# Loads of the first two pairs issued from ScalarE's queue as well as SyncE's, in a fused linear-attention and gated-MLP kernel

## The chip, the cores and the metric

The kernel runs on one core of a Trainium2 chip. The metric is device time in microseconds (us). A core has a matrix engine (TensorE, in the profile PE; its weight loads are PEld), a vector engine (VectorE, DVE), an engine for activation functions (ScalarE, ACT), GpSimd (POOL) and SyncE (SP), which here only starts transfers. Each engine runs its own instructions in order. A transfer (DMA) is started by an instruction on an engine's queue and then carried by 16 DMA engines.

## The reference

The first half is a recurrence over 768 time steps for 4 batches and 8 heads, with a state of 48 by 48 that decays per row; the second is a two-layer network on the result, with the activation h * cos(h).

```python
for t in range(S):                       # q, k, v, alpha: [4, 8, 768, 48], float32
    state = alpha[:, :, t, :, None] * state + einsum('bhd,bhe->bhde', k[:, :, t], v[:, :, t])
    y[:, :, t] = einsum('bhd,bhde->bhe', q[:, :, t], state)
x = y.transpose(0, 2, 1, 3).reshape(3072, 384)
h = x @ w_in                             # [384, 2048]
return (h * cos(h)) @ w_out              # [2048, 384], float32
```

## The kernel before

Time is cut into 12 pairs (J = 0 to 11, three for each batch) of 256 steps. A partition holds two neighbouring steps (e = 0 and 1) of all heads, and each half of the partitions is a chunk of its own. For each pair the kernel

- loads a (alpha), k, q and v, each as a tile of 128 partitions with 8 heads of 96 float32 (`load`, L102 to L116; one transfer of 384 KB each),
- takes the logarithm of a on ScalarE (`ln`, L139), sums it over time on PE by matmuls with triangular masks (`cums0` and `cums`, L155 and L167) and takes exponentials of the sums and of their negatives on ScalarE (`exps`, L200, and `icp`, L192),
- scales k and q by these (`scale_k`, L212, `scale_q`, L216), casts v to bfloat16 (`cast_v`, L219) and copies it into a second layout (`stack_v_pe`, L235, `evict_vs`, L239),
- forms the outer products that feed the state (`outer`, L291), transposes q and k (`trans`, L260, `evict_T`, L266), forms scores (L274), masks them (L279), and builds y (`yT`, L340),
- runs the network: `mlp1` (L359), the cosine on ScalarE (`cosine`, L365), the product on VectorE (`gate`, L370), `mlp2` (L387), the copy out of PSUM and the store.

The logarithm and exponential share one set of ScalarE's function tables, the cosine has another; `act_set` (L136) loads the first set where it isn't in place.

All steps are issued in an order that is written out by hand. `PLAN` has a line for each kind of step and on it a number for each pair; the steps are sorted by these numbers and issued in that order, so the numbers set the order of the instructions on every engine, and nothing else. A suffix gives the engine (A for ScalarE, D for VectorE). Before the change the loads of pairs 0 and 1 stand in the order k0, a0, a1, k1, v0, q0, q1, v1, all on SyncE's queue. `IDLE` puts matmuls on zeros (`idle`, L411) into PE's order, 21 of them at its start. The loads of pair 2 and later stand on SyncE's queue as well; the load of a for pair 2 waits for `yT` of pair 1 (`GATES`). The weights w1 and w2 are loaded from GpSimd's queue (L121, L127).

Of the kernel before, what the change touches and what calls it, by code (L numbers as in the profile page):

```python
# [16 lines left out]
def kernel(  # L17
# [10 lines left out]
    nc = tc.nc  # L28
# [73 lines left out]
    def load(nm, J):  # L102
        b, g = J // NJB, J % NJB
        t = sb.tile([C, H, 2, D], FP, tag=nm, name=nm, bufs=BUF["a" if nm == "a" else "in"])
        dma = nc.sync.dma_start(
            out=t.rearrange("p h e d -> p h (e d)"),
            in_=src[nm][b, :, g * T2 : (g + 1) * T2, :].rearrange("h (p e) d -> p h (e d)", e=2),
        )
        if (nm, J) in AFTER:
            tc.add_manual_dep(dma.ins, AFTER[nm, J].ins.name,  # L110
                              mybir.DependencyInfo(mybir.DependencyClass.Sync, mybir.DependencyReason.DATA),
                              reason="inputs of later pairs stay behind the weights")
        if nm == "a":
            a_sb[J] = t
        else:
            kqv[nm, J] = t  # L116
# [290 lines left out]
    def idle(n):  # L407
# [6 lines left out]
    mults = {"DVE": nc.vector, "POOL": nc.gpsimd}  # L414
    steps = {
        "load": lambda J, nm: load(nm, J), "w1": load_w1, "w2": load_w2,
        "mula": mul_a, "ln": ln, "cums0": cums0, "cums": cums, "sub": sub, "icp": icp, "exps": exps, "eb": session,
        "sk": lambda J, e, eng="POOL": scale_k(J, e, mults[eng]), "sq": lambda J, e, eng="POOL": scale_q(J, e, mults[eng]),
# [7 lines left out]


    PLAN = {
        "load a": "1320 1974 27415 27985 34270 40270 43270 54870 67336 68770 70970 93397",
        "load k": "750 2544 28555 37270 46270 52480 58570 69470 72470 85140 91627 113474",  # L430
        "load q": "5250 6750 29125 38770 48970 56370 57870 60070 78470 84570 87104 96187",
        "load v": "3750 8250 35770 41770 51910 61570 67906 73970 75470 85710 95267 96757",
        "w1": "15334 12769 17804 16954",
        "w2": "11919 20284 19434 21134",
        "mula": "- - - 36680 41180 47582 54280 61956 76220 87867 79850 105765",
# [61 lines left out]
    for key, line in PLAN.items():  # L497
        kind, *rest = key.split()
        for J, word in enumerate(line.split()):
            if word != "-":  # L500
                t, _, eng = word.partition(":")
# [38 lines left out]
```

## Time and profile before

| | |
|---|---|
| median of 3 runs | 189.61 us (189.58 to 190.51) |
| profiled execution: its own time | 189.73 us |
| profiled execution: span from first to last instruction | 187.7 us |
| mean granted TensorE clock | 0.997 of full speed |
| busy: PE, DVE, ACT, POOL | 177.2, 134.3, 125.3, 77.4 us |
| data moved | 29.47 MB, a mean of 157 GB/s |

The profile is of one execution. A line of a timeline has the start, the time taken, the engine, the line of the code, the operation with its output and input tiles, the number of instructions that are merged, and in brackets how long the engine had been idle before it and what released it. SPq and ACTq are the issuing instructions of a queue, and their time is that of the issue, not of the transfer. A line of the chain of waits has a start, a time and the work that the end of the program goes back to at that moment. A line of the DMA view with a queue's name has packets, megabytes and the share of 16 DMA engines.

### The profile page before, as it was taken

What the parts mean: (1) busy time and instruction counts of PE and PEld (TensorE: products, weight loads), DVE (VectorE), ACT (ScalarE), POOL (GpSimd) and SP (SyncE); (2) the same over time, 40 slices, a digit from 0 to 9 for tenths busy, and PEclk for the clock granted to TensorE, in tenths of its full rate; (3) what the DMA queues carried; (4) which work ended last, traced back from release to release, by engine and by line L of the source; (5) the groups of instructions that cost most, each with busy time, mean ns of one, the idle gap of its engine ahead of it and who ended that gap; (6) DMA issues with size and microseconds to landing.
All of it is one profiled execution on the core that took longest, in us unless ns stands there. A gap on an engine that the chain in (4) does not pass through costs nothing.

```text
span 187.7 us, 5795 instructions
## 1 busy us (share of the span) xinstructions
PE 177.2 (94%) x2471; PEld 126.7 (67%) x2474; DVE 134.3 (72%) x184; ACT 125.3 (67%) x161; POOL 77.4 (41%) x110
## 2 busy tenths in 40 slices
PE   7997799998999999999999999999999999999990
PEld 2444678664577776775688668686776786776880
DVE  7069775589799899589657986885876666573550
ACT  2466876899598977788577999728956182372520
POOL 5059610257664733783894068830540310100000
PEclk9999999999999999999999999999999999999998
DMA  6999999999959988996799943600042005501303
GB/s 152 261 256 154 185 203 236 255 264 265 249 137 302 265 184 217 265 268 166 195 280 259 216 106 90 166 0 3 3 114 73 0 21 124 128 1 45 84 0 84
DMA packets 60537, 29.47 MB, mean 157 GB/s; under 512 B 51424, under 2 KB 60512, under 8 KB 60512
## 3 DMA queue, kind: packets, MB, share of 16 engines
q1 hardware_dynamic: 56640, 25.86, 59.8%
q0 software_dynamic: 3712, 3.15, 11.0%
q8 instruction: 19, 0.31, 0.7%
q10 hardware_dynamic: 160, 0.10, 0.2%
q14 instruction: 6, 0.05, 0.1%
HBM read 25.17 MB, written 4.72 MB: 159 GB/s over the span
## 4 chain that ended last, share of the span: by engine, by line
PE 71%; ACT 16%; DVE 7%; issue 3%; DVEq 0%
PE h_ps L359 31%; PE o_ps L387 23%; PE idle_ps L411 5%; PE y_ps L340 3%; ACT c_sb L365 3%; ACT qkT L266 3%; DVE gsb L370 3%; PE T_ps L260 2%; ACT cp L200 2%; ACT L136 2%; ACT L365 2%; PE A_ps L274 2%; PE U_ps L291 2%; ACT lna L141 2%; ACT icp L192 2%
## 5 line engine op out<-in xcount | busy, mean ns | idle before, releaser
L370 DVE TENSOR_TENSOR gsb<-h_ps,c_sb 128x1024 bf16<-128x1024 f32 x48 | 58.1, 1221 | 22.3 <-ACT c_sb L365 21.5
L365 ACT ACTIVATE c_sb<-h_ps,halfpi 128x1024 bf16<-128x1024 f32 x48 | 53.0, 1113 | 27.4 <-PE h_ps L359 23.4
L359 PE MATMUL h_ps<-xT,w 128*128 128x256 bf16 x576 | 66.7, 273 | 1.4 <-issue 0.6
L387 PE MATMUL o_ps<-w,gsb 128*128 128x384 bf16 x368 | 66.7, 326 | 0.0
L359 PEld LDWEIGHTS <-w 128*128 128x128 bf16 x576 | 55.6, 98 | 10.4 <-issue 1.9
L387 PEld LDWEIGHTS <-gsb 128*128 128x128 bf16 x368 | 33.8, 98 | 21.2 <-DVE gsb L370 0.6
L313 POOL TENSOR_TENSOR un<-us,c 128x384 bf16<-128x384 f32 x20 | 16.8, 843 | 40.3 <-DVE us L305 33.9
L279 DVE TENSOR_TENSOR A_sb<-A_ps,msk 128x1024 bf16<-128x1024 f32 x24 | 28.9, 1216 | 1.3 <-PE A_ps L274 1.3
L212 POOL TENSOR_TENSOR kh<-k,icp 128x384 bf16<-128x384 f32 x17 | 16.9, 999 | 8.7 <-ACT icp L192 8.7
L216 POOL TENSOR_TENSOR qh<-q,cp 128x384 bf16<-128x384 f32 x15 | 15.4, 1032 | 10.9 <-ACT cp L200 10.9
L149 POOL TENSOR_TENSOR a<-a 128x384 f32<-128x384 f32 x9 | 9.3, 1037 | 12.9 <-DMA a<-in_alpha_dram 12.9
L411 PE MATMUL idle_ps<-zeros 128*128 128x512 bf16 x42 | 12.7, 445 | 1.6 <-DVE zeros L52 1.2
L219 POOL CAST vp<-v 128x768 bf16<-128x768 f32 x12 | 9.9, 824 | 9.0 <-DMA v<-in_v_dram 8.9
L141 ACT ACTIVATE lna<-a 128x768 bf16<-128x768 f32 x12 | 10.2, 846 | 4.5 <-DMA a<-in_alpha_dram 4.5
L136 ACT ACT_TABLE_LOAD x9 | 11.5, 1283 | 0.9 <-PEq L524 0.7
L266 ACT COPY qkT<-T_ps 128x1024 bf16<-128x1024 bf16 x8 | 8.0, 1016 | 6.2 <-PE T_ps L260 3.8
L266 DVE COPY qkT<-T_ps 128x1024 bf16<-128x1024 bf16 x16 | 10.8, 682 | 1.3 <-ACT qkT L266 1.3
L365 ACT ACT_TABLE_LOAD x9 | 11.5, 1283 | 0.2
L305 DVE TENSOR_TENSOR us<-U_ps,un 128x384 f32<-128x384 f32 x16 | 8.7, 550 | 3.8 <-PE U_ps L291 2.8
L396 DVE COPY o_sb<-o_ps 128x384 f32<-128x384 f32 x12 | 6.6, 552 | 6.6 <-PE o_ps L387 6.6
L274 PE MATMUL A_ps<-qkT 48*128 48x128 bf16 x192 | 9.2, 218 | 1.0 <-ACT vs L239 0.6
L396 ACT COPY o_sb<-o_ps 128x384 f32<-128x384 f32 x11 | 5.3, 478 | 7.1 <-PE o_ps L387 5.2
(69 smaller groups left out, 155.1 us busy)
## 6 DMA issues: line engine op xcount, KB each, us to landing
k<-in_k_dram SPq DMA_DIRECT2D x12, 384.0 KB, 5.5
a<-in_alpha_dram SPq DMA_DIRECT2D x12, 384.0 KB, 5.9
v<-in_v_dram SPq DMA_DIRECT2D x12, 384.0 KB, 6.2
q<-in_q_dram SPq DMA_DIRECT2D x12, 384.0 KB, 6.0
out_dram<-o_sb SPq DMA_DIRECT2D x46, 96.0 KB, 2.7
vs<-vp SPq DMA_DIRECT2D x36, 64.0 KB, 2.0
w<-in_moe_w_out_dram POOLq DMA_DIRECT2D x4, 384.0 KB, 9.9
w<-in_moe_w_in_dram POOLq DMA_DIRECT2D x4, 384.0 KB, 7.0
```

Source lines behind the costliest of these rows:

```text
L136: nc.scalar.preload_act_table_set("natural_log_exp_and_others")
L141: nc.scalar.activation(out=lna_t[J % NL][:, :, :, 0:D].rearrange("p e h d -> p h e d"), in_=a_sb.pop(J), func=AF.Ln)
L212: eng.tensor_tensor(out=kh_t[J % NQ][:, e, :, 0:D], in0=kqv["k", J][:, :, e], in1=icp_, op=ALU.mult)
L216: eng.tensor_tensor(out=qh_t[J % NQ][:, e, :, 0:D], in0=kqv["q", J][:, :, e], in1=cp, op=ALU.mult)
L266: copy(out=qkT_sb[J][:, c], in_=T_ps[J][:, c].rearrange("r n e s -> r n (e s)"))
L279: nc.vector.tensor_tensor(out=A_sb[J][:, c].rearrange("s a p t -> s (a p) t"), in0=A_ps.pop((J, c)).rearrange("s a p t -> s (a p) t"), in1 ...
L313: nc.gpsimd.tensor_tensor(out=u, in0=U_sum.pop(n), in1=c2_sb[J][:, :, c].unsqueeze(3).to_broadcast([C, NP, 2, D]), op=ALU.mult)
L359: nc.tensor.matmul(h_ps[J, u][:, f, :], w1[:, kk, ft * C : (ft + 1) * C], xT[J][:, kk, :], start=(kk == 0), stop=(kk == KT - 1))
L365: nc.scalar.activation(out=c_sb[J, u], in_=h_ps[J, u], func=AF.Sin, bias=halfpi, scale=1.0)
L370: nc.vector.tensor_tensor(out=gsb[J][:, u * FW : (u + 1) * FW], in0=h_ps.pop((J, u)), in1=c_sb.pop((J, u)), op=ALU.mult)
L387: nc.tensor.matmul(o_ps[J, c][:, 0:DM], gsb[J][:, ft, c * C : (c + 1) * C], w2[:, ft], start=(ft == 0), stop=(ft == NF - 1))
L411: nc.tensor.matmul(idle_ps[0], zeros[:, 0:C], zeros, start=True, stop=True)
```

## The change

The first two pairs' k and v are issued from ScalarE's queue, and all eight loads of these pairs get numbers at the head of the plan, in the order k0, a0, k1, a1, v0, q0, v1, q1. In the sorted order the four on ScalarE's queue then stand ahead of the first step that uses ScalarE, and with it ahead of its first table load. All other steps keep their numbers.

```diff
     def load(nm, J):
         b, g = J // NJB, J % NJB
         t = sb.tile([C, H, 2, D], FP, tag=nm, name=nm, bufs=BUF["a" if nm == "a" else "in"])
-        dma = nc.sync.dma_start(
+        eng = nc.scalar if J < 2 and nm in "kv" else nc.sync
+        dma = eng.dma_start(
             out=t.rearrange("p h e d -> p h (e d)"),
             in_=src[nm][b, :, g * T2 : (g + 1) * T2, :].rearrange("h (p e) d -> p h (e d)", e=2),
         )
...
-        "load a": "1320 1974 27415 27985 34270 40270 43270 54870 67336 68770 70970 93397",
-        "load k": "750 2544 28555 37270 46270 52480 58570 69470 72470 85140 91627 113474",
-        "load q": "5250 6750 29125 38770 48970 56370 57870 60070 78470 84570 87104 96187",
-        "load v": "3750 8250 35770 41770 51910 61570 67906 73970 75470 85710 95267 96757",
+        "load a": "752 754 27415 27985 34270 40270 43270 54870 67336 68770 70970 93397",
+        "load k": "751 753 28555 37270 46270 52480 58570 69470 72470 85140 91627 113474",
+        "load q": "756 758 29125 38770 48970 56370 57870 60070 78470 84570 87104 96187",
+        "load v": "755 757 35770 41770 51910 61570 67906 73970 75470 85710 95267 96757",
```

## The prediction

> **What bounds the kernel now.** The page comes first: PE is busy for 94% of the span and the granted clock is at 9 tenths or more up to the last slice, so a change at the start counts if it moves the moment from which PE runs without pause. I therefore read the chain of waits for the first 28 us.
>
> ```profile
> 1.20 7.00 PE idle_ps L411 x21
> 8.19 0.65 PE cums_h L155 x4
> 8.84 0.18 PE cums_h L167 x8
> 9.02 0.24 PE idle_ps L411
> 9.26 0.65 PE cums_h L155 x4
> 9.91 0.19 PE cums_h L167 x8
> 10.10 0.02 issue
> 10.13 0.49 ACT cp L200
> 10.62 0.39 ACT icp L192
> 11.01 0.02 issue
> 11.03 1.10 DVE kh L212 x2
> ```
>
> No transfer is in it. The 21 filler matmuls hold PE until 8.2 us, then the cumulative sums of pair 0 and pair 1 follow, and ScalarE's second exponential (10.13) waits for pair 1's sums. From there to the end of the span the chain is computation. So earlier data cannot shorten it; later data can lengthen it. How late may data be? The next view is the timeline of ScalarE and of SyncE's queue.
>
> ```profile
> 0.74 1.28 ACT L136 ACT_TABLE_LOAD   x1 [0.74 <-PEq L524]
> 5.86 0.84 ACT L141 ACTIVATE lna<-a 128x768 bf16<-128x768 f32 x1 [3.83 <-DMA a<-in_alpha_dram]
> 7.36 0.84 ACT L141 ACTIVATE lna<-a 128x768 bf16<-128x768 f32 x1 [0.67 <-DMA a<-in_alpha_dram]
> ...
> 0.74 0.42 SPq L105 DMA_DIRECT2D k<-in_k_dram  x1
> 1.23 1.60 SPq L105 DMA_DIRECT2D a<-in_alpha_dram  x2
> 2.87 1.25 SPq L105 DMA_DIRECT2D k<-in_k_dram  x1
> 4.16 1.44 SPq L105 DMA_DIRECT2D v<-in_v_dram  x1
> 5.65 2.93 SPq L105 DMA_DIRECT2D q<-in_q_dram  x2
> 8.62 1.44 SPq L105 DMA_DIRECT2D v<-in_v_dram  x1
> ```
>
> The logarithm of pair 0 ends at 6.70 and is used at 8.03; that of pair 1 ends at 8.20 and is used at 9.10. The slack is 1.33 and 0.90 us. The table load is over at 2.02, well ahead of the first data.
>
> The queue's lines show something else: an issue takes 0.42 us when nothing is queued, but 1.25 to 1.44 from the third or fourth on. The issuing engine is held. The DMA view, cut at the ends of the fourth, fifth and sixth issue (4.12, 5.60 and 7.10 us), shows why:
>
> ```profile
> q1 hardware_dynamic: 1486, 0.56, 53.5%
> q1 hardware_dynamic: 2508, 0.95, 72.9%
> q1 hardware_dynamic: 3546, 1.34, 84.4%
> ```
>
> A load is 1,024 packets of 384 bytes. Issued less moved is 4096 - 1486 = 2610, then 5120 - 2508 = 2612, then 6144 - 3546 = 2598: the queue takes about 2,600 packets (2.5 loads) and the next issue ends only as packets leave. They leave at (3546 - 2508) / 1.5 = 692 per us, 262 GB/s, one load each 1.5 us. Issue start plus time to landing gives the landings: k0 4.36, a0 5.8, a1 7.3, k1 8.87, v0 10.4, q0 11.85, q1 13.3, v1 14.8.
>
> **What the change does, part by part.** In the compiled order ScalarE begins with k0, k1, v0, v1, and only then come the table load and the two logarithms. SyncE begins with a0, a1, q0, q1. Engine orders on PE, VectorE and GpSimd stay as they were. Nothing is added or removed in work; eight issues are spread over two queues, and ScalarE gets four of them ahead of its first computation.
>
> *The transfers.* The bytes are the same and the stretch 4 to 10 us already runs at 261 to 262 GB/s, so the last of the eight lands at about 14.8 as before. The order changes. Both queues begin at 0.74 and have equal loads, so I take them to fill the stream in turn: k0 with a0, k1 with a1, v0 with q0, v1 with q1, each couple landing at the time of the later one. Then a0 5.8 as now, a1 8.87 instead of 7.3, k0 and k1 early enough (k is first used at 9.58), v0 11.85 instead of 10.4, q0 as now, q1 14.8 instead of 13.3. The bounds for a1 are its old place (7.3) and the fourth place (8.87); equal sharing is nearest to the fourth, and I take it. The Trainium skill says the same of the gain, against the change: in "DMA: Bandwidth & Descriptors", section "Issuing engines are not separate DMA queues", DMAs from any engine run on the same 16 DMA engines and interleave, and a second issuer saves only sequencer time. By that rule the stream would stay at its 262 GB/s, as the sum has it; no run here yet shows two load queues together.
>
> *ScalarE's time.* If its queue can hold 2,600 packets of its own, v1's issue ends when 4096 - 2600 = 1,496 packets of this queue have left. With equal shares that is 2,992 in all, at 5.60 + (2992 - 2508) / 692 = 6.30 us. The table load (1.28, nothing hides it now) ends at 7.6, pair 0's logarithm at 8.44. PE has been ready for it at 8.03, so pair 0's sums are 0.43 late and end, with the one filler matmul, at 8.46 + 1.07 = 9.53. Pair 1's logarithm starts on a1 at 8.87 and ends at 9.71; its sums start at 9.73 instead of 9.10. That is +0.63, and it covers the 0.43.
>
> *What follows.* Pair 1's sums release ScalarE's second exponential at 10.76 instead of 10.13. The products kh, on VectorE, end at 12.76 instead of 12.13. GpSimd's cast of v0 starts on v0 at 11.87 and takes 0.82: 12.70, so PE's outer products, which need both, begin at 12.78; the two of them that ran ahead at 11.77 now run here, about 0.02. VectorE's product for pair 1's q, 14.37 before, comes at 15.0, behind q1's 14.8. GpSimd's weight issues stand behind the cast and two small products, and go 0.6 later along with their users (the first weight matmul is at 22.25). The sum is +0.65 us. Below, +0.43 (a1 early, ScalarE the limit); above, +0.9 (ScalarE's fourth issue also waits for one of SyncE's, or the shared stream loses some rate). The chain behind it has no slack that would give it back.
>
> The profiled execution took 189.73 with a span of 187.7, 0.12 over the median of 189.61. From its span the forecast is 188.35 us, and from the median 190.26: 190.3.
>
> **The rivals.**
>
> *One shared allowance: much slower.* The 2,600 packets could be the limit of both queues together. The issues then end as in the SyncE column now, in turn, and ScalarE's fourth is the seventh or the eighth: 8.58 or 10.06. Add the table load (1.29) and pair 0's logarithm (0.84): PE starts the sums at 10.74 or 12.2 instead of 8.03, +2.71 or +4.2, nothing in between hides it, and the time is 192.3 or 193.8. It decides as soon as v1's issue ends later than about 6.7. For it: the trace has one queue only under load, so whose limit it is stays unseen. Against it: the page counts the two queues apart (q1 and q10), and at 183.8 to 184.5, where SyncE and ScalarE both issue stores, ScalarE's took 565 and 550 ns and SyncE's 547 to 717, against a median of 595 for all SyncE's stores; neither stood behind the other for a whole issue. The Trainium skill speaks for it: "Perfetto Trace Analysis", section "DMA Instruction — HWDGE (DVE, Sync)", has one descriptor generator shared by the sequencers and locked until an issue's descriptors are all made. A full lock of this kind is not what the store rows show. I give the case 30 in 100: 17 for the seventh place, 13 for the eighth. In between (a partly shared limit, +0.95 to +2.4) I put 7.
>
> *Hidden: no change.* If SyncE's queue is served first, a1 keeps its old landing, and if ScalarE's fourth issue ends by 5.9, its table load and logarithms lie inside the slack: 189.6. It needs both; 4 in 100.
>
> *Faster.* Two queues could draw more than 262 GB/s. But the page's best slices are 302 and 280, and the chain's start is filler matmuls, not data; a gain over 0.95 us would have to come from a better order later on, for which no row speaks: 188.6 or less, 4 in 100.
>
> **How the numbers follow.** The forecast has 55 in 100, with its own range from 190.0 to 190.5; 3 of the 55 lie above the half per cent. A measurement of this kernel tells about 0.5% from no change, 0.95 us here, so the forecast itself is a slowdown that counts as the same. Same: 52 + 4 = 56. Slower: 3 + 30 + 7 = 40. Faster: 4. The range leaves out the eighth place (13) and the faster case (4): from 189.6 to 192.9, which takes in the seventh place with 0.6 for its error.
>
> **What would show it.** In the profile after, ScalarE's queue should have four issues from 0.74, the last ending at 6.3 to 6.7; the table load behind it; the logarithms at about 7.6 and 8.87, the second still waiting for a; the second exponential at 10.76; the weight matmuls from 22.9. If the fourth issue ends at 8.5 or later and the second logarithm follows the first without a wait, the shared allowance is right and the price is ScalarE's. If the logarithms are at 5.9 and 7.4, the change is hidden. A total below 189 would make the whole reading of the start wrong.

## The result, and the profile after

The changed kernel takes 191.93 us (median of 4 runs, 191.65 to 192.72) against 189.88 for the kernel before (4 runs), a ratio of 1.0115 with a 95% interval of 1.0084 to 1.0147: 1.2% slower, 2.05 us. Timed again later beside other kernels it gave 1.0124 (1.0092 to 1.0155). The forecast was 190.3, with a range from 189.6 to 192.9. The direction held; the size was a third of the measured one. By the prediction's own line of 0.5% between the same and slower this is slower, to which it gave 40 in 100 and not the larger share. That the range held is partly luck: its upper part was there for the rival of one shared allowance, which did not come true, and the forecast's own range, 190.0 to 190.5, missed.

The profiled execution of the change has a span of 190.9 us at its own time of 192.72, the longest of its four; the other three have spans of 189.9 to 190.2. First the timeline of SyncE's queue and of ScalarE in the changed kernel (start, time taken, engine, line, operation, tiles):

```profile
0.75 1.07 SPq L106 DMA_DIRECT2D a<-in_alpha_dram  x2
1.86 3.96 SPq L106 DMA_DIRECT2D q<-in_q_dram  x2
...
0.74 1.25 ACTq L106 DMA_DIRECT2D k<-in_k_dram  x2
2.02 4.48 ACTq L106 DMA_DIRECT2D v<-in_v_dram  x2
6.53 1.28 ACT L137 ACT_TABLE_LOAD   x1 [6.53 <-issue]
7.82 1.64 ACT L142 ACTIVATE lna<-a 128x768 bf16<-128x768 f32 x2
9.74 0.49 ACT L193 ACTIVATE icp<-cums_h 128x384 f32<-128x384 f32 x1 [0.28 <-PE cums_h L168]
10.81 0.49 ACT L201 ACTIVATE cp<-cums_h 128x384 f32<-128x384 f32 x1 [0.58 <-PE cums_h L168]
```

ScalarE's four issues end at 6.50, the table load follows at 6.53, and the second exponential starts at 10.81 instead of 10.13. That is the forecast almost to the tenth (6.3 to 6.7, and 10.76). The two logarithms run without a wait between them, though; the forecast had the second one wait for its a.

Next, the chain of waits of the changed kernel from the second exponential to the first weight matmul (start, time, what):

```profile
10.81 0.49 ACT cp L201
11.30 0.39 ACT icp L193
11.69 0.02 issue
11.71 0.80 DVE kh L213 x2
12.51 0.14 issue
12.65 1.18 DVE kh L213
13.83 0.97 DVE qh L217 x2
14.80 0.47 DVE us L308
15.27 1.67 DVE qh L217 x2
16.94 0.68 issue
17.62 0.56 DVE us L306
18.17 0.14 issue
18.31 0.40 PE A_ps L275 x8
...
24.21 0.04 issue
24.25 2.79 PE h_ps L360 x24
```

Before, the chain went through PE and ScalarE here; now it goes through VectorE. One product kh takes 1.18 us, where such a product took about 0.55; the second state sum (L306) starts at 17.62 instead of 15.95, and the scores of pair 0, which wait for it, at 18.31 instead of 16.30. The first weight matmul is at 24.25 instead of 22.25: here the loss stands at 2.00 us.

The scores did not wait for this sum before. These are the scores, ScalarE's copy of v into the second layout (`evict_vs`) and the second state sum, first in the kernel before and then in the changed one:

```profile
15.44 0.81 ACT L239 CAST vs<-vs_ps 128x768 bf16<-128x768 f32 x1
15.95 0.54 DVE L305 TENSOR_TENSOR us<-U_ps,un 128x384 f32<-128x384 f32 x1
16.30 0.40 PE L274 MATMUL A_ps<-qkT 48*128 48x128 bf16 x8 [0.62 <-ACT vs L239]
...
16.77 0.81 ACT L240 CAST vs<-vs_ps 128x768 bf16<-128x768 f32 x1
17.62 0.55 DVE L306 TENSOR_TENSOR us<-U_ps,un 128x384 f32<-128x384 f32 x1
18.31 0.40 PE L275 MATMUL A_ps<-qkT 48*128 48x128 bf16 x8 [1.31 <-DVE us L306]
```

Before, the scores started 0.05 us after the copy, while the sum still ran; after, 0.14 us behind the sum, and the copy had long been done. The kernel's code lets the tiles U_ps, vs_ps, T_ps and A_ps take turns in three PSUM buffers (tag "h", `bufs=3`), so the scores seem to have got another of them, although every engine computes in the same order as before. Why the build chose so is open. The profiles fall into two groups. In the kernel before and in experiments 3 and 8 the scores wait for the copy; in the changed kernel and in experiments 1, 2, 4, 5, 6 and 7 they wait for the sum. From the scores to the first weight matmul it is 5.94 to 5.95 us in all of them, so the whole loss is there when the scores start. By these rows the copy is 1.3 us late; the wait for the sum in its place makes the other 0.7, an estimate (18.31 against 17.58 + 0.05).

What GpSimd did at that time, in its timeline:

```profile
12.56 0.86 POOL L220 CAST vp<-v 128x768 bf16<-128x768 f32 x1 [9.38 <-DMA v<-in_v_dram]
13.39 1.00 POOL L245 TENSOR_TENSOR c<-cp,dmask 128x16 f32<-128x16 f32 x2
14.34 0.93 POOL L128 DMA_DIRECT2D w<-in_moe_w_out_dram  x1
15.26 0.75 POOL L122 DMA_DIRECT2D w<-in_moe_w_in_dram  x1
16.02 0.85 POOL L314 TENSOR_TENSOR un<-us,c 128x384 bf16<-128x384 f32 x1
```

The cast waits for pair 0's v until 12.56 (10.42 before), and from then on GpSimd is never free until the state product `un` at 16.02, which was at 14.61. PE's outer products wait for this cast (13.47, where most of them stood at 12.18 before; PE is idle for 0.95 us ahead of them), and the copy of v stands behind them on PE and ScalarE.

Behind 24.25 the distance stays between 2.0 and 2.5 until 98 us. There PE pauses in mid-layer with no releaser (0.62 us before, 1.36 after), which makes the 3.2 us of the two profiled spans. That pause differs from one execution to the next, from 0.6 to 1.6 in most of the profiles below and absent in one; the 2.05 of the medians is nearly the 2.00 of the first 24 us.

### The profile page after: what moved, and what is told of

Same layout as the page of the kernel before. It is cut to its first block, busy times and chain, and to the rows that moved or that the text cites. A ratio compares the mean times of both kernels' runs of the same rounds, so it can differ in the third digit from the quotient of the medians.

```text
span 190.9 us, 5796 instructions
## 1 busy us (share of the span) xinstructions
PE 177.3 (93%) x2471; PEld 126.7 (66%) x2474; DVE 136.2 (71%) x184; ACT 125.3 (66%) x161; POOL 77.1 (40%) x110
## 3 DMA queue, kind: packets, MB, share of 16 engines
q10 hardware_dynamic: 4320, 1.67, 4.1%
## 4 chain that ended last, share of the span: by engine, by line
PE 61%; ACT 12%; DVE 9%; DMA 5%; issue 4%; ACTq 3%; SPq 2%; POOL 2%; POOLq 0%; DVEq 0%
PE h_ps L360 27%; PE o_ps L388 22%; DMA v<-in_v_dram 5%; PE y_ps L341 3%; ACTq L106 3%; DVE gsb L371 3%; ACT c_sb L366 2%; DVE qh L217 2%; PE A_ps L275 2%; ACT L137 2%; PE T_ps L261 2%; DVE kh L213 2%; ACT qkT L267 2%; PE U_ps L292 1%; ACT cp L201 1%
## 5 line engine op out<-in xcount | busy, mean ns | idle before, releaser
L306 DVE TENSOR_TENSOR us<-U_ps,un 128x384 f32<-128x384 f32 x16 | 8.7, 550 | 3.8 <-PE U_ps L292 2.8
L213 DVE TENSOR_TENSOR kh<-k,icp 128x384 bf16<-128x384 f32 x7 | 5.2, 765 | 7.2 <-ACT icp L193 7.2
```

The lines of the kernel that those rows point to most:

```text
L213: eng.tensor_tensor(out=kh_t[J % NQ][:, e, :, 0:D], in0=kqv["k", J][:, :, e], in1=icp_, op=ALU.mult)
```

## The experiments

Two theories went in. **Late operands**: ScalarE's late logarithms cost 0.7, the late landing of pair 0's v more, and the work beside it on VectorE and GpSimd the rest. **ScalarE held**: all of it comes from ScalarE being kept by its own issues until 6.5. Each kernel was timed against the kernel before; "weights at" is the start of the first weight matmul in its profile (before 22.25, changed 24.25).

**1. The table load ahead of the four issues** (the changed kernel with one line more)

```diff
+        act_set("exp")
         for _, _, kind, args in sorted(order, key=lambda x: x[:2]):
```

> The changed kernel with ScalarE's table load moved ahead of its four load issues. Theory 'late v': the change costs its 2.0 us in three steps, ScalarE held until 6.5 (+0.7 at the second exponential), pair 0's v landing at 12.5 instead of 10.4 so that the outer products start at 13.47 instead of 12.18, and the cast of that v then running beside VectorE's products, which take longer (+0.7). The table load is hidden here, but the four issues start 1.3 us later, so v lands no earlier: outer products at 13.5 to 14.2, time 191.6 to 192.5. Rival 'ScalarE held': all of the loss comes from ScalarE's logarithms starting late; they start at 6.5 to 7.2 here, inside or near the old slack, and the time falls to 189.9 to 190.4.

Measured 191.64 us, ratio 1.0067 (1.0044 to 1.0090); weights at 24.01. ScalarE's timeline:

```profile
0.74 1.28 ACT L137 ACT_TABLE_LOAD   x1 [0.74 <-PEq L526]
0.78 1.21 ACTq L106 DMA_DIRECT2D k<-in_k_dram  x2
2.02 4.52 ACTq L106 DMA_DIRECT2D v<-in_v_dram  x2
6.58 0.84 ACT L142 ACTIVATE lna<-a 128x768 bf16<-128x768 f32 x1 [4.56 <-issue]
8.69 0.84 ACT L142 ACTIVATE lna<-a 128x768 bf16<-128x768 f32 x1 [1.27 <-DMA a<-in_alpha_dram]
```

The issues did not start later, as I had expected: they run beside the table load. So the table load is hidden and pair 0's logarithm is 1.2 us earlier, yet pair 1's waits for its a until 8.69 and the second exponential comes at 10.61 instead of 10.81. Of the 0.68 us at this point, 0.2 belong to ScalarE's issues and 0.5 to a1, which stands behind k0 and k1 in the shared stream. The cast of v was still at 12.70. "ScalarE held" falls: it expected 189.9 to 190.4.

**2. Half of the queues: only k on ScalarE's**

```diff
-        eng = nc.scalar if J < 2 and nm in "kv" else nc.sync
+        eng = nc.scalar if J < 2 and nm == "k" else nc.sync
```

with SyncE's loads in the order a0, a1, v0, q0, q1, v1 (two numbers of the plan changed for it).

> Half of the change: only the two loads of k on ScalarE's queue; SyncE's has a0, a1, v0, q0, q1, v1. ScalarE's issues should end near 2.0 and the table load near 3.3. Late v: v0 is the third on SyncE's queue and lands near 10, the logarithms are not held, 189.5 to 190.4. ScalarE held: the same, as ScalarE is free early. A third rival, 'two queues slow the stream' (two load queues move less per us than one): v0 and the later loads land later than 10.4 and the time is above 190.5.

Measured 190.65, ratio 1.0014 (0.9992 to 1.0035); weights at 23.21. ScalarE's two issues end at 1.98 and its table load at 3.29. The cast of v0 starts at 10.73. That is later than 10.4 and the time is above 190.5, as the third rival said, but the stream was not slower: from 6 to 12 us it moved 261 to 262 GB/s, as in the kernel before (261). The second exponential is at 10.75, since a1's logarithm started only at 8.71. The time is a little over the expected 190.4; the scores waited for the state sum here, until 17.27, 0.34 us longer than for the copy of v (16.88) by the same reckoning as above.

**3. The order alone, all on SyncE's queue**

```diff
-        eng = nc.scalar if J < 2 and nm in "kv" else nc.sync
+        eng = nc.sync
```

> The other half of the change: the eight loads in the new order k0, a0, k1, a1, v0, q0, v1, q1, but all on SyncE's queue, so ScalarE issues nothing. a1 lands at 8.87 instead of 7.3 and v0 at 10.4 as before. Late v: second exponential at 10.7 to 10.8 because of a1 (+0.63), outer products at 12.8, time 190.3 to 190.9. ScalarE held: 189.9, the same as before, since ScalarE is not held by issues.

Measured 190.80, ratio 1.0021 (0.9996 to 1.0045); weights at 23.15. a1's logarithm starts at 9.11, the second exponential at 11.03, the cast of v0 at 10.66 as early as ever. So putting k1 ahead of a1 costs 0.90 us at the first weight matmul without any second queue; about 0.2 of it is a start of the whole stream that was later in this profile (a0's logarithm at 6.09 instead of 5.86). The medians put it at 0.6 with an interval that touches zero.

**4. v0 and q0 exchanged between the queues** (ScalarE issues as many loads)

```diff
-        eng = nc.scalar if J < 2 and nm in "kv" else nc.sync
+        eng = nc.scalar if (nm, J) in (("k", 0), ("k", 1), ("q", 0), ("v", 1)) else nc.sync
```

The two loads have each other's number in the plan as well.

> The changed kernel with the queues of pair 0's v and q exchanged: SyncE has a0, a1, v0, q1 and ScalarE k0, k1, q0, v1, so ScalarE issues as many loads as in the change and is held as long (to 6.5), while v0 stands third on the queue that got ahead. Late v: v0 lands near 10.7 instead of 12.5, outer products at 12.85 instead of 13.47, and GpSimd's cast is over before most of VectorE's products: 190.4 to 191.2. ScalarE held: no change against the changed kernel, 191.7 to 192.2.

Measured 191.07, ratio 1.0032 (1.0011 to 1.0053); weights at 23.53. ScalarE's issues end at 6.63, as late as in the change, and its logarithms start at 7.95; the cast starts at 11.95, 0.6 earlier than in the change (10.7 had been expected), and 0.7 of the 2.0 us at the first weight matmul are back. The interval of the ratio lies below that of the change, and "ScalarE held", which expected 191.7 to 192.2, falls here too.

**5. The changed kernel again, and its second state sum ahead of one product**

> The changed kernel itself, timed beside the next three on the same chip: 191.6 to 192.2 and a ratio to the kernel before of 1.007 to 1.011.

Measured 192.39, ratio 1.0124 (1.0092 to 1.0155), a little above both expectations.

```diff
-        "sq 0": "12160:D 14753:D 40150:D ...
+        "sq 0": "12160:D 15560:D 40150:D ...
```

> The changed kernel with one VectorE product (pair 1's q, e = 0) moved behind the second state sum of pair 0 (L306). In the profile of the change this product took 2.04 us beside GpSimd's work instead of 0.55, and the state sum behind it, which frees the PSUM buffer that the scores of pair 0 wait for, started at 17.62 although its operand from GpSimd was there at 16.87. Theory 'late operands' with a collision on the path: the sum starts at 16.9, the scores at 17.6 instead of 18.31, and the time falls by 0.4 to 0.7 against the changed kernel. Rival 'off the path' (the scores wait for something else as well): less than 0.2.

Measured 191.62, ratio 1.0098 (1.0062 to 1.0133): the intervals overlap, so this run does not decide. In its profile the scores are at 18.17 against 18.55 in the repeat of the change, with the cast at 12.76 and 12.80. But the encounter of the cast with kh fell the other way round here: the cast took 1.22 us and the three products kh 1.50 together, where the change has 0.86 and 2.12. With the longer cast the copy of v ended only at 18.13, so the scores could hardly have come earlier by either wait.

**6. v0 late, without a second queue** (the kernel before with pair 0's q and v exchanged; one queue, a1 where it was)

```diff
-        "load q": "5250 6750 ...
+        "load q": "3750 6750 ...
-        "load v": "3750 8250 ...
+        "load v": "5250 8250 ...
```

> The kernel before, all loads on SyncE's queue, with pair 0's v and q exchanged: v lands sixth, near 11.87, instead of fifth, near 10.4. ScalarE issues nothing and a1 lands as before. Late operands: GpSimd's cast starts at 11.9, the outer products at 12.75 instead of 12.18, and the time rises by 0.5 to 0.9. Rival 'ScalarE and a1 alone': v has room until 11.3 at least and what is lost is given back, within 0.2 of the kernel before.

Measured 191.38, ratio 1.0086 (1.0054 to 1.0119): 1.2 us by the medians and 1.6 by the ratio, more than the 0.5 to 0.9 us expected. The chain of waits:

```profile
10.26 0.49 ACT cp L200
...
12.10 1.18 DVE kh L212
13.28 0.97 DVE qh L216 x2
14.26 0.47 DVE us L307
14.72 1.67 DVE qh L216 x2
16.39 0.68 issue
17.07 0.56 DVE us L305
17.62 0.14 issue
17.76 0.40 PE A_ps L274 x8
```

The second exponential is at 10.26, 0.13 after that of the kernel before (its whole start is 0.12 later). From kh on, the chain has the durations of the changed kernel one for one: 1.18, 0.97, 0.47, 1.67, and the pause ahead of the state sum. The cast started at 12.03 here, beside the product kh at 12.10. Weights at 23.71, +1.46. A cast 1.6 us later, on the old queue, with ScalarE untouched, brings three quarters of the loss. It does so in the same two parts: the outer products are at 12.92 and the copy of v ends at 17.02, 0.8 later than before, which is what had been expected; the scores start 0.7 after that, because in this kernel too they wait for the sum. Exchanging two numbers of loads was enough to change that wait.

**7. GpSimd's state product ahead of its first two weight issues** (in the changed kernel)

```diff
-        "w1": "15334 12769 17804 16954",
-        "w2": "11919 20284 19434 21134",
+        "w1": "15334 14466 17804 16954",
+        "w2": "14465 20284 19434 21134",
```

> The changed kernel with GpSimd's first two weight issues (0.93 and 0.75 us) moved behind its first state product (L314). In the change GpSimd is busy without a pause from the late cast to this product, cast 12.56, two small products, two issues, product 16.02 to 16.87, and the second state sum, the release of a PSUM buffer and the scores of pair 0 (18.31) stand behind it. Theory 'late operands', with GpSimd's queue as the carrier: the product runs at 15.3 instead of 16.02, the state sum at 16.3 to 16.9, the scores at 17.0 to 17.6 and the time falls by 0.5 to 1.0 against the changed kernel, unless the weights then land too late for the first weight matmul (they go 0.9 later). Rival 'PE carries it' (the late outer products alone): the scores stay at 18.0 to 18.3 and the time within 0.2.

Measured 193.33, ratio 1.0174 (1.0149 to 1.0199). The step went as expected, the total did not fall. Lines of VectorE's and PE's timelines:

```profile
15.21 1.65 DVE L217 TENSOR_TENSOR qh<-q,cp 128x384 bf16<-128x384 f32 x2
16.78 0.55 DVE L306 TENSOR_TENSOR us<-U_ps,un 128x384 f32<-128x384 f32 x1
...
17.48 0.40 PE L275 MATMUL A_ps<-qkT 48*128 48x128 bf16 x8 [0.45 <-DVE us L306]
...
23.42 1.47 PE L360 MATMUL h_ps<-xT,w 128*128 128x256 bf16 x12 [0.51 <-ACT xT L351]
25.78 1.48 PE L360 MATMUL h_ps<-xT,w 128*128 128x256 bf16 x12 [0.89 <-DMA w<-in_moe_w_in_dram]
28.24 1.48 PE L360 MATMUL h_ps<-xT,w 128*128 128x256 bf16 x12 [0.97 <-DMA w<-in_moe_w_in_dram]
```

`un` starts at 15.43 instead of 16.02, the two products qh take 1.65 instead of 2.50, the state sum starts at 16.78 instead of 17.62, the scores at 17.48 instead of 18.31, the first weight matmul at 23.42: 0.83 us of the 2.00 are back. Then PE waits 0.89 and 0.97 us for weights, which now come later, and loses more than it had won, as the expectation had allowed for. The scores come earlier than the 18.0 to 18.3 of "PE carries it". So GpSimd's queue carries the state sum that the scores of this kernel wait for; and these two weight issues cannot be moved back so far without a price. The run says nothing of the late outer products, which are at 13.49 here as well.

**8. A candidate: a0 and a1 first, all on SyncE's queue, fewer fillers**

```diff
-        "load a": "1320 1974 ...
-        "load k": "750 2544 ...
+        "load a": "750 751 ...
+        "load k": "752 753 ...
-    IDLE = [(1501, 21), (7915, 1), (9416, 8), ...
+    IDLE = [(1501, 12), (7915, 1), (9416, 8), ...
```

> A candidate: all loads on SyncE's queue in the order a0, a1, k0, k1, v0, q0, q1, v1, with 12 filler matmuls at PE's start instead of 21. a0 lands at 4.4, a1 at 5.9, so the sums can start near 6.0 instead of 8.03 and the second exponential near 8.1 instead of 10.13; v0 still lands at 10.4, so the outer products come at 11.3 instead of 12.18. Late operands (the landing of each operand against its use sets the start): faster than before by 0.7 to 1.1. Rival 'PE's fillers are needed': fewer fillers leave PE at its slow rate (0.43 us for a filler matmul, as in the first 5 us) for longer, and nothing is gained.

Measured 188.86 us, ratio 0.9942 (0.9918 to 0.9966): faster than both kernels. The logarithms start at 4.65 and 6.16, the second exponential at 8.08, the outer products at 11.58. The profile does not show the gain: the profiled execution was the slowest of its twelve (190.08 us), and its first weight matmul is at 22.92, 0.67 later than before. Behind an idle PE of 1.79 us its fillers stand about 0.43 us apart and its transposes take 0.61 us, and the granted clock was 0.50 from 13 to 15 us, where it was 1.00 in the kernel before. Its mean clock was 0.986; the other eleven executions had 0.995 to 1.000. A second kernel fills this gap with 16 fillers instead of 8 at (9416, 8):

> The candidate with a0 and a1 first, and 16 instead of 8 filler matmuls behind pair 1's sums. In the candidate's profile PE stood idle for 1.79 us ahead of the outer products, and the fillers behind it took about 0.43 us apart again and the transposes 0.61 instead of 0.41 us. If that gap is what slows PE: 0.21 us fillers and 0.41 us transposes, the first weight matmul near 22.2 or earlier in the profile, and 188.2 to 188.8. If not: the same as the candidate, 188.6 to 189.1.

Measured 189.48, ratio 0.9969 (0.9951 to 0.9986). The granted clock is 1.00 there, the transposes take 0.41 again and the weights are at 21.66, 0.59 ahead of the kernel before, as expected, but the time lies above both ranges, 188.2 to 188.8 and 188.6 to 189.1, and is no better than the candidate's; the two intervals overlap. By the mean clocks above, the candidate's other executions had little of that slow stretch, so there was little for the fillers to win. Whether they cost something is open.

## Why the prediction was right or wrong, point by point

- *ScalarE held until 6.3, pair 1's sums 0.63 late*: nearly right in its numbers, 6.50 and 0.68 at the second exponential. Both limits that the prediction named, ScalarE's time and a1's landing, fell together here: ScalarE, free at 8.66, found a1 there, and in experiment 1, where it was free earlier, it waited for a1 until 8.69.
- *Each queue has an allowance of 2,600 packets of its own*: right. When SyncE's fourth issue ended at 5.82, its queue had 4096 - 1463 = 2633 packets left, and when ScalarE's ended at 6.50, 4096 - 1359 = 2737, by the DMA view of the changed kernel cut at these times:

```profile
q1 hardware_dynamic: 1463, 0.56, 41.4%
...
q10 hardware_dynamic: 1359, 0.52, 34.2%
```

  The rival of one shared allowance (192.3 or 193.8) is out, though the measured time lies near its first figure: the right total would have come from a wrong reason. With it goes the reading by the Trainium skill, "Perfetto Trace Analysis", section "DMA Instruction — HWDGE (DVE, Sync)", if the lock it tells of were held for a whole issue: SyncE's first two issues took 1.07 us beside ScalarE's first two (1.25 us), and 1.06 us in experiment 8, where SyncE issued alone.
- *Equal shares, v0 at 11.85*: this step failed in its size, by 0.7; the cast started at 12.56. It goes through the sum one for one: the outer products are at 13.47 instead of the forecast's 12.78, and the copy of v behind them is 1.3 late instead of 0.65. The shares are equal only once both queues run. SyncE's packets started first: at 4.0 us its queue had moved 865 packets and ScalarE's 394, although the issues began at 0.75 and 0.74. From 5.6 to 13.0 they moved 3934 - 1367 = 2567 and 3601 - 1073 = 2528, evenly, as the Trainium skill has it ("DMA: Bandwidth & Descriptors", section "Queues, rings and completion order": each DMA engine goes round the queues that have work). The start is in no row of before.
- *The sum of +0.65 goes through unchanged*: this step failed. I wrote that the engine orders stay as they were, and they did, but I took the waits for unchanged with them, and what stands ahead of the prediction says that the numbers of the plan set the order "and nothing else". The releaser of the scores changed, from the copy of v to the second state sum, and that is 0.7 of the 2.0 us by the estimate above. The sum is late because of a queue that I let go "0.6 later along with their users": behind GpSimd's cast stand two small products, two weight issues and then the state product, which the sum needs. Before, the cast was done at 11.24 and this queue waited for ScalarE (12.24); in the change the cast ends at 13.42 and all the rest queues up behind it without a gap. Experiment 7 shows that this queue carried the sum. Experiment 6 gives a late v without a second queue, with both parts in it; no run has the late v with the old wait, so the two parts are split by the rows alone.
- *Durations from the profile before hold after*: failed too. A VectorE product with two operands in SBUF took 0.55 us in most places, but 1.18 and 2.04 where GpSimd was computing beside it. In the first 28 us of before this happened once (1.19, at the second product of pair 1's q), and the scores did not wait for what stood behind it; the change and experiment 6 moved the cast onto the product kh. A row of before showed the effect, and I gave it no part. The Trainium skill describes it in "SBUF — State Buffer", section "SBUF: two separate sides": a VectorE instruction with two inputs in SBUF and a GpSimd instruction that reads SBUF need the same pair of ports, which is locked for a whole instruction, and the later one waits. The traces agree for the first encounter: the cast began at 12.56 and the product at 12.65, and the product ended at 13.83, 0.41 us after the cast; in experiment 5 the product began first (12.75 against 12.76), and the cast took longer. For the second (2.04 us, beside a state product of 0.85 and weight issues) the runs don't show which of GpSimd's instructions held it; the product just ahead of it took 0.54 beside a weight issue.
- *Nothing can become faster, since no transfer is in the chain*: right for this change. Experiment 8 shows the other side: fewer fillers and earlier landings of the two a's together bring about 1.1 us (ratio 0.9942); no run has one without the other.

The +2.00 at the first weight matmul thus comes from the order of the landings, not from the time that ScalarE spends on issuing. v0 is late enough to hold PE's outer products (1.3) and, through GpSimd and VectorE, the state sum that the scores now wait for (0.7, the estimate). a1 behind both k's costs 0.90 by itself (experiment 3); in the change the outer products wait for v0 alone, so it is hidden behind v0: from experiment 6 to the change the cast comes 0.53 later and the scores 0.55. With the table load ahead of the issues (experiment 1) 0.24 comes back.

## What to carry to other kernels

A second issuing queue added no bandwidth to a stream that was full already (261 to 262 GB/s from 6 to 12 us with one queue and with two), and it changed which load lands when; check each load's landing against its first use, and put those needed first at the head, whatever queue they are on. When an operand lands late, follow every engine queue it passes to the next buffer that is released, not only the one on the present chain. After a change, compare what releases each step, and not only the order of the steps: here the exchange of two load numbers gave the scores another releaser. A duration in a profile holds only beside the neighbours it was measured with: where VectorE reads two operands from SBUF while GpSimd computes, look for the same line's longest time, not its mean.

## What the runs showed of the hardware that was not expected

- A transfer issued on ScalarE's queue does not wait for a table load that stands ahead of it: the load ran from 0.74 to 2.02 and the first two issues from 0.78 to 1.99 (experiment 1). The other way round the load waits for the issues, 6.53 in the change.
- With both queues issuing at 0.74, the packets of ScalarE's queue came later: 1 had moved by 2.83 us, against 321 of SyncE's.
- PE's pause near 98 to 103 us has no releaser in any profile. Packets of the instruction queue (q8) move at that time, but they don't tell the profiles apart: between 96 and 102 us there were one in the changed kernel (1.36 us of pause), two in the kernel before (0.62) and two in the one profile without the pause. What PE waits for is open.
